# Earlier requests for raw weights, a third buffer for v pairs, and the early normalisation on GpSimd

## The chip, the core and the metric

The kernel runs on one core of a Trainium2 chip. The metric is the device time of one execution in microseconds, the median of several runs. The engines are TensorE (PE in the profile, with its weight loads as PEld), VectorE (DVE), ScalarE (ACT), GpSimd (POOL) and SyncE (SP), which here only issues DMAs. Each engine works through its own queue in order.

## What is computed

Attention with a forget bias, then two gated layers, all in fp32 accuracy (B = 4, H = 8, S = 576, D = 64; 2304 tokens of 512):

```python
scores = scale * np.matmul(q, k.transpose(0, 1, 3, 2))
cum = np.cumsum(np.maximum(s, 0.0), axis=-1)
bias = -(cum[:, :, :, None] - cum[:, :, None, :])
scores = np.where(causal, -1000000000.0, scores + np.minimum(bias, 0.0))
attn = np.exp(scores - np.max(scores, axis=-1, keepdims=True))
attn = attn / (np.sum(attn, axis=-1, keepdims=True) + 1e-09)
x = np.matmul(attn, v)                                   # then heads side by side: 2304 x 512
x = (1.0 / (1.0 + np.exp(-(x @ w_gate))) * (x @ w_val)) @ moe_w_out      # 512 -> 1536 -> 512
h = x @ w_in                                                             # 512 -> 2048
out = (h - np.tanh(h)) @ moe2_w_out                                      # -> 512
```

## The kernel before

Only the first of the kernel's stages is touched: attention together with the first gated layer, up to about 560 us of the span. The attention is cut into units, one for each batch entry, head and half G of the queries; the 32 units of G = 0 (256 queries) come first. A unit of G = 0 has two steps, t = 0 with 128 keys and t = 1 with 256, so steps 0 to 63 belong to G = 0. The first N32 = 16 units (steps 0 to 31) compute with plain fp32 operands; later units split each operand into two fp32r parts.

The order on every engine is written out by hand, in the loop over steps at line 533. Iteration i holds: on DVE eps(i-1), ttr(i) (the scores read out of PSUM with the bias and the row minimum), recip(i-1) and norm(i-1); on ACT the read-out of the transposed p of step i-2, then exp(i); on POOL mask(i+2), an affine select on the bias tile cbc; on PE qk(i+1), then the transposes tr(i-1), then pv once a unit is complete. From iteration 20 on PE also gets blocks of the first gated layer, called moe here: 12 matmuls for one 128-column weight and one group of 256 queries. Two of them go into each iteration from 20 to 28, one into those from 29 to 34. What moe writes is read out by ACT (tanh) and DVE (gt), and stored by SP in flush.

The weights come as raw 64-bit words, 24 loads of 512 KB, into tiles raw, and are turned into pairs of fp32r tiles (w00h, w00l and so on) by the class Conversion. One call of tick k does three things: for weight k-2 an ACT copy to the h part (line 109) and a POOL subtract to the l part (line 110), for weight k-1 two DVE instructions that join the words (lines 79, 80), for weight k an ACT scale that reads the raw tile (line 75). Three ticks come before the loop, then one at the end of iterations 1, 3, 5, 7, 9, 11 and 13, then one in each iteration from 15 on. Raw tiles have three buffers, and the load of weight k+1 is requested at tick k:

```python
while self.loaded < min(len(self.jobs), max(self.ticks - 1, 0) + self.nraw, most):
    self.raw[i] = self.pool.tile([128, 1024], U, tag="raw", name="raw", bufs=self.nraw)
    SP.dma_start(out=self.raw[i], in_=self.jobs[i][0])
```

SP issues in program order the q and k of a unit (kq, lines 255 and 259), the bias rows of a unit (cbc, two DMAs, line 276), the v of two heads (vpair, two DMAs, line 282), the raw weights (line 96) and the stores of gt (line 476). A load waits in SP's queue until its buffer is free, and everything behind it waits too. load_vc(u+2) asks for a vpair at the first step of an even unit u; vpair has two buffers in pool ld, so it needs pv of unit u-1 to be over:

```python
d["v"] = ld.tile([128, 2, 2, D], F, tag="v", name="vpair")
for a in range(2):
    SP.dma_start(out=d["v"][:, :, a], in_=v[b, h + a, :, 0:nj])
```

Two tiles pth and ptl in pool pt hold p for units from 16 on. POOL clears them at iterations 14 and 15; nothing else uses them before step 32. For those units split_kq makes kl, qs and split_v makes vs on POOL.

Of the kernel before, what the change touches and what calls it, by code (L numbers as in the profile page):

```python
# [8 lines left out]
F = mybir.dt.float32  # L9
R = mybir.dt.float32r  # L10
U = mybir.dt.uint32
# [3 lines left out]
B, H, S, D = 4, 8, 576, 64  # L15
# [12 lines left out]
NK = 3  # L28
# [3 lines left out]
RAW0 = 2  # L32
N32 = 16
# [14 lines left out]
def width(t):  # L48
    return Q0[t] + 128
# [6 lines left out]
def NORM(G, t):  # L56
    return "pool" if t > 2 else "dve"
# [3 lines left out]
def attention_moe_moe2(ctx: ExitStack, tc: tile.TileContext, kqT, v, s, wg, wv, wo, win, wo2, out):  # L61
    nc = tc.nc
    PE, ACT, DVE, POOL, SP = nc.tensor, nc.scalar, nc.vector, nc.gpsimd, nc.sync
# [19 lines left out]
    class Conversion:  # L83


        def __init__(self, pool, jobs, nraw, ntmp, first=99):
            self.pool, self.jobs, self.nraw, self.ntmp = pool, jobs, nraw, ntmp
            self.loaded = self.ticks = 0
            self.raw, self.tmp = {}, {}
            self.load(first)  # L90

        def load(self, most=99):
            while self.loaded < min(len(self.jobs), max(self.ticks - 1, 0) + self.nraw, most):
                i = self.loaded
                self.raw[i] = self.pool.tile([128, 1024], U, tag="raw", name="raw", bufs=self.nraw)
                SP.dma_start(out=self.raw[i], in_=self.jobs[i][0])
                self.loaded += 1

# [130 lines left out]
    pt = a_right.enter_context(tc.tile_pool(name="pt", bufs=1, side="right"))  # L229
    ld = a_right.enter_context(tc.tile_pool(name="ld", bufs=2, side="right"))  # L230
    at = a_right.enter_context(tc.tile_pool(name="at", bufs=2, side="right"))
    sm = a_right.enter_context(tc.tile_pool(name="sm", bufs=4, side="right"))
    cv = a_right.enter_context(tc.tile_pool(name="cv", bufs=2, side="right"))

    make_identity(nc, ident)
    NPT = 1
    pts = [[pt.tile([128, 5, 320], R, name=f"pt{p}{i}") for p in "hl"] for i in range(NPT)]

    units = [(b, G, h) for G in range(2) for b in range(B) for h in range(H)]
    steps = [(u, t) for u, (b, G, h) in enumerate(units) for t in GRP[G][2]]  # L240
# [2 lines left out]
    def shape(u):  # L243
        b, G, h = units[u]
        q0, qw, ts = GRP[G]
        return b, h, q0, q0 + qw, qw, 2 if G == 0 else 5
# [15 lines left out]
    def load_vc(u):  # L262
        if u >= len(units):
            return
        b, h, q0, kw, qw, nj = shape(u)
        d = U_[u]
        if u >= N32:
            d["v"] = ld.tile([128, 5, D], F, tag="v", name="vraw")[:, :nj]
        elif h % 2:
            d["v"] = U_[u - 1]["v"]  # L270
        else:
            d["v"] = ld.tile([128, 2, 2, D], F, tag="v", name="vpair")
        d["c"] = c = ld.tile([128, CW], F, tag="c", name="cbc", bufs=3)
        for t in GRP[units[u][1]][2]:
            k0 = 288 if t == 4 else 0
            SP.dma_start(out=c[:, CO[t]:CO[t] + width(t) - k0],
                         in_=cscr[b * H + h, k0:width(t)].partition_broadcast(128))
        if u >= N32:
            SP.dma_start(out=d["v"], in_=v[b, h, :, 0:nj])
        elif h % 2 == 0:  # L280
            for a in range(2):
                SP.dma_start(out=d["v"][:, :, a], in_=v[b, h + a, :, 0:nj])
# [98 lines left out]
    def norm(i):  # L381
        if 0 <= i < n:
            e = T_[i]
            u, t = steps[i]
            if NORM(units[u][1], t) == "pool":
                POOL.tensor_scalar(out=e["sp"], in0=e["sp"], scalar1=e["r"], scalar2=1.0, op0=ALU.mult, op1=ALU.mult)
            else:
                DVE.tensor_scalar(out=e["sp"], in0=e["sp"], scalar1=e["r"], scalar2=None, op0=ALU.mult)  # L388
# [121 lines left out]
    cq = [((wg, wv)[g][m].bitcast(U).rearrange("p k c -> p (k c)"), *wgv[g][m]) for m in range(M1) for g in range(2)]  # L510
# [1 line left out]
    sraw = at.tile([32, S], F, tag="sp", name="sraw", bufs=NSP)  # L512
    SP.dma_start(out=sraw, in_=s.rearrange("b h s -> (b h) s"))
    load_kq(0)
    cvt = Conversion(cv, cq, 3, 3, RAW0)
    zt = at.tile([32, S], F, tag="sp", name="zt", bufs=NSP)
    cum = at.tile([32, S], F, tag="sp", name="cumsum", bufs=NSP)
    DVE.memset(zt, 0.0)
# [1 line left out]
    DVE.tensor_tensor_scan(out=cum, data0=sraw, data1=zt, initial=0.0, op0=ALU.add, op1=ALU.add)  # L520
    SP.dma_start(out=cscr, in_=cum)
    load_vc(0)
    load_kq(1)
    load_vc(1)
    for _ in range(PRE):
        cvt.tick()
# [6 lines left out]
    for i in range(n + LN + 1):  # L533
        u, t = steps[i] if i < n else (None, None)
        b, G, h = units[u] if i < n else (None, None, None)
        first = i < n and t == GRP[G][2][0]
        if first and h == 0:
            left = (16 if G == 0 else 24) + LN + 2 + (2 if u + H == len(units) else 0)
        k = -(-len(mq) // left) if i < n else 0
# [49 lines left out]
            moe(*mq.pop(0))  # L589
        if CONV_AT(i):  # L590
            cvt.tick()
        if i in (N32 - 2, N32 - 1):
            POOL.memset(pts[0][i % 2].bitcast(F), 0.0)
    for x in xq:
        xsum(*x)
        xsplit(x[0])
# [16 lines left out]
    cvt = Conversion(cv2, [(wo[m * 128:(m + 1) * 128].bitcast(U), *won[m]) for m in range(M1)], 4, 3)  # L613
# [45 lines left out]
    jobs = [(win[m].bitcast(U).rearrange("p k c -> p (k c)"), *winn[m]) for m in range(M2)]  # L659
    cv3 = b_right.enter_context(tc.tile_pool(name="cv3", bufs=2, side="right"))  # L660
    cvt = Conversion(cv3, jobs, 2, 3)
# [114 lines left out]
    def wload(p):  # L776
# [3 lines left out]
    cvt = PairConversion(cv4, [("right", [wo2[m * 128:(m + 1) * 128].bitcast(U) for m in (p, p + MP)], p)  # L780
                               for p in range(MP)], dst, POOL)
# [60 lines left out]
    for i, (s, p) in enumerate(dsteps):  # L842
# [7 lines left out]
        for n in OORD:  # L850
            g, f = OG[n], OW[n]
# [54 lines left out]
```

## Time and profile before

| | before |
|---|---|
| median of 3 runs | 1117.04 us (1116.92 to 1117.46) |
| the profiled execution, its own time | 1119.6 us |
| its span | 1117.8 us |
| PE busy | 1061.5 us (95%) |
| DVE, ACT, POOL busy | 681.7, 546.0, 458.7 us |
| chain that ended last | PE 84%, DMA 6%, DVE 4%, ACT 2% |

The page cuts the span into 40 slices of 28 us. PE is busy in nine tenths or more of every slice from the fifth to the 39th; the first four read 3, 8, 6 and 8 tenths. What the change touches lies in these first slices.

### The profile page before, as it was taken

The numbers are of one execution on the slowest core, as the hardware profiler recorded it, in microseconds if no ns is written. First come the engines' busy times: TensorE is split into PE (matmuls) and PEld (weight loads), VectorE is DVE, ScalarE is ACT, GpSimd is POOL, SyncE is SP. The second block draws the span as 40 slices with busy tenths as digits, with TensorE's granted clock in tenths as the row PEclk, the third lists the DMA queues.
The fourth block names the chain that finished last, engine by engine and source line by source line (L and its number), as shares of the span: only waits on it lengthen the run. The fifth ranks groups of instructions, "written<-read, shape, count | busy, mean of one in ns | idle before, by whom it ended". The sixth has DMA issues, their size and how long they took to land.

```text
span 1117.8 us, 21882 instructions
## 1 busy us (share of the span) xinstructions
PE 1061.5 (95%) x7528; PEld 1023.6 (92%) x7528; DVE 681.7 (61%) x1654; ACT 546.0 (49%) x1286; POOL 458.7 (41%) x580
## 2 busy tenths in 40 slices
PE   3868999999999999999999999999999999999998
PEld 1547899989999999998999999999999999999997
DVE  4764856577867677764545654244444436778876
ACT  3543656566756566664434443344444333334333
POOL 2442645467756656662321211013333323354442
PEclk9999999999999999999999999999999999999999
DMA  5545545565756465550755563244465668644433
GB/s 186 163 139 166 153 128 146 159 186 150 178 143 173 126 185 136 157 139 24 234 177 182 168 193 111 57 143 142 135 233 197 253 230 328 236 118 140 143 89 109
DMA packets 123888, 180.38 MB, mean 161 GB/s; under 512 B 16960, under 2 KB 102464, under 8 KB 122496
## 3 DMA queue, kind: packets, MB, share of 16 engines
q1 hardware_dynamic: 123776, 178.98, 52.7%
q8 instruction: 59, 0.97, 0.4%
q14 instruction: 53, 0.43, 0.1%
HBM read 131.93 MB, written 47.00 MB: 160 GB/s over the span
## 4 chain that ended last, share of the span: by engine, by line
PE 84%; DMA 6%; DVE 4%; ACT 2%; issue 2%; SPq 1%; POOL 0%; DVEq 0%; ACTq 0%; POOLq 0%
PE bank L490 8%; PE bank L491 8%; PE bank L494 8%; PE bank L722 6%; PE bank L725 6%; PE bank L721 6%; PE bank L857 5%; PE bank L855 5%; PE bank L856 5%; PE bank L438 5%; PE bank L683 4%; PE bank L684 4%; PE bank L687 4%; PE bank L400 4%; PE bank L349 2%; DMA raw<-in_wv 2%
## 5 line engine op out<-in xcount | busy, mean ns | idle before, releaser
L857 PE MATMUL bank<-wo,sl 128*128 128x256 f32 x504 | 142.6, 283 | 0.8 <-DVE sl L770 0.8
L855 PE MATMUL bank<-wo,sh 128*128 128x256 f32 x504 | 141.9, 281 | 0.0
L856 PE MATMUL bank<-wo,sh 128*128 128x256 f32 x504 | 141.8, 281 | 0.0
L721 PE MATMUL bank<-yh,big 128*128 128x288 f32 x512 | 139.6, 294 | 0.0
L722 PE MATMUL bank<-yh,big 128*128 128x288 f32 x512 | 139.5, 295 | 0.0
L418 ACT ACTIVATE pth<-bank 128x512 fp32r<-128x512 f32 (+2 forms) x128 | 59.5, 465 | 144.0 <-PE bank L438 86.7
L728 DVE TENSOR_TENSOR th<-bank,th 128x288 f32<-128x288 f32 x128 | 57.4, 456 | 113.9 <-ACT th L727 112.3
L400 PE MATMUL bank<-ident,sp 128*128 128x128 f32 (+1 forms) x480 | 78.1, 272 | 37.0 <-DVE sp L388 15.8
L419 DVE TENSOR_TENSOR ptl<-bank,pth 128x512 fp32r<-128x512 f32 (+2 forms) x128 | 66.7, 521 | 66.5 <-PE bank L438 39.2
L400 PEld LDWEIGHTS bank<-ident,sp 128*128 128x128 f32 (+1 forms) x480 | 52.7, 143 | 55.2 <-issue 24.1
L370 ACT ACTIVATE sp<-sp,nm 128x576 f32<-128x576 f32 (+2 forms) x160 | 95.7, 598 | 13.6 <-DVE nm L363 13.6
L727 ACT ACTIVATE th<-bank 128x288 f32<-128x288 f32 x128 | 51.9, 410 | 99.8 <-PE bank L725 98.4
L857 PEld LDWEIGHTS bank<-wo,sl 128*128 128x128 f32 x504 | 95.3, 189 | 1.7 <-DVE sl L770 1.2
L722 PEld LDWEIGHTS bank<-yh,big 128*128 128x128 f32 x512 | 96.1, 188 | 0.0
L721 PEld LDWEIGHTS bank<-yh,big 128*128 128x128 f32 x512 | 96.0, 187 | 0.0
L856 PEld LDWEIGHTS bank<-wo,sh 128*128 128x128 f32 x504 | 95.3, 189 | 0.0
L855 PEld LDWEIGHTS bank<-wo,sh 128*128 128x128 f32 x504 | 95.3, 189 | 0.0
L725 PE MATMUL bank<-yl,big 128*128 128x288 f32 x512 | 88.6, 294 | 0.0
L765 POOL TENSOR_TENSOR s<-g 128x256 f32<-128x256 f32 (+1 forms) x40 | 37.1, 926 | 124.6 <-DMA g<-h 95.0
L629 DVE TENSOR_TENSOR gl<-g,gh 128x384 fp32r<-128x384 f32 x72 | 39.9, 557 | 75.9 <-PE bank L687 47.6
L388 DVE TENSOR_SCALAR sp<-sp,r 128x128 f32<-128x128 f32 (+1 forms) x96 | 81.2, 845 | 3.4
L363 DVE CUSTOM_DVE_ANT_0 sp<-bank,cbc 128x288 f32<-128x288 f32 (+2 forms) x160 | 76.1, 476 | 4.2 <-POOL cbc L327 2.6
(358 smaller groups left out, 3163.3 us busy)
## 6 DMA issues: line engine op xcount, KB each, us to landing
h<-th SPq DMA_DIRECT2D x128, 144.0 KB, 2.3
kq<-in_kq SPq DMA_DIRECT2D x32, 448.0 KB, 3.8
raw<-in_wo SPq DMA_DIRECT2D x28, 512.0 KB, 4.8
g<-g SPq DMA_DIRECT2D x72, 192.0 KB, 2.6
g<-h SPq DMA_DIRECT2D x72, 128.0 KB, 2.3
w<-wst SPq DMA_DIRECT2D x5, 1792.0 KB, 6.4
wo<-w SPq DMA_DIRECT2D x5, 1792.0 KB, 8.5
cbc<-cum SPq DMA_DIRECT2D x32, 256.0 KB, 5.5
```

The costliest lines, as they stand in the source:

```text
L370: ACT.activation(out=e["sp"], in_=e["sp"], func=AF.Exp, scale=-1.0, bias=e["m"], accum_out=e["sum"])
L388: DVE.tensor_scalar(out=e["sp"], in0=e["sp"], scalar1=e["r"], scalar2=None, op0=ALU.mult)
L400: PE.transpose(ps[:, j, :], e["sp"][p0:128, c:c + 128], ident[p0:128, p0:128])
L490: PE.matmul(ps, wh[:, c], xh[:, k], start=(k == 0), stop=False)
L491: PE.matmul(ps, wl[:, c], xh[:, k], start=False, stop=False)
L494: PE.matmul(ps, wh[:, c], xl[:, k], start=False, stop=(k == KD - 1))
L721: PE.matmul(ps, wh[:, c], Y_[blk][k][0], start=(k == 0), stop=False)
L722: PE.matmul(ps, wl[:, c], Y_[blk][k][0], start=False, stop=False)
L725: PE.matmul(ps, wh[:, c], Y_[blk][k][1], start=False, stop=(k == KD - 1))
L855: PE.matmul(o, sh[:, g, c], w[:, 0, f], start=(p == 0 and t == 0), stop=False)
L856: PE.matmul(o, sh[:, g, c], w[:, 1, f], start=False, stop=False)
L857: PE.matmul(o, sl[:, g, c], w[:, 0, f], start=False, stop=(p == MP - 1 and t == nt - 1))
```

## The change

Four edits in the first stage:

- Conversion for these weights gets two further buffers, nraw + extra = 5. The load of weight k+3 is requested at tick k. Buffers 3 and 4 of each five (rawx) lie in pool pt, in the memory of the later pth and ptl.
- pth and ptl are therefore made, and cleared on POOL, at iterations 30 and 31, after the last conversion.
- vpair moves to pool at, into the three buffers of tag kl, which units from 16 on use for kl. Tag v of pool ld is left to the v of units from 16 on.
- norm of the first 16 units (32 instructions) is issued on POOL, in front of mask(i+2), in the form that later steps with t > 2 already use there.

```diff
-        def __init__(self, pool, jobs, nraw, ntmp, first=99):
-            self.pool, self.jobs, self.nraw, self.ntmp = pool, jobs, nraw, ntmp
+        def __init__(self, pool, jobs, nraw, ntmp, first=99, more=None, extra=0):
+            self.pool, self.jobs, self.nraw, self.ntmp = pool, jobs, nraw + extra, ntmp
+            self.more, self.own = more, nraw
...
-                self.raw[i] = self.pool.tile([128, 1024], U, tag="raw", name="raw", bufs=self.nraw)
+                k = i % self.nraw - self.own
+                if k < 0:
+                    self.raw[i] = self.pool.tile([128, 1024], U, tag="raw", name="raw", bufs=self.own)
+                else:
+                    self.raw[i] = self.more.tile([128, 1024], U, tag=f"pt{'hl'[k]}", name="rawx")
...
-            d["v"] = ld.tile([128, 2, 2, D], F, tag="v", name="vpair")
+            d["v"] = at.tile([128, 2, 2, D], F, tag="kl", name="vpair", bufs=NK)
...
-            if NORM(units[u][1], t) == "pool":
+            if u < N32 or NORM(units[u][1], t) == "pool":
...
-    cvt = Conversion(cv, cq, 3, 3, RAW0)
+    cvt = Conversion(cv, cq, 3, 3, RAW0, pt, 2)
...
-        if i in (N32 - 2, N32 - 1):
-            POOL.memset(pts[0][i % 2].bitcast(F), 0.0)
+        if i in (2 * N32 - 2, 2 * N32 - 1):
+            assert cvt.done(len(cq) - 1)
+            p = "hl"[i % 2]
+            pts[0].append(pt.tile([128, 5, 320], R, tag=f"pt{p}", name=f"pt{p}0"))
+            POOL.memset(pts[0][-1].bitcast(F), 0.0)
```

The order of instructions on PE is the same in both kernels, and so is that on ACT apart from the names of two buffers. On DVE 32 norms go. SP and POOL are shown at three places; in the changed file the line numbers are five higher, and eight from the loop's end on.

On SP, at the start of the program: the q and k of units 1 to 3 (kq), bias rows (cbc), v pairs and raw weights. Before:

```order
L255 DMA kq_201<-in_kq 64x512
L276 DMA cbc<-cum 128x128
L276 DMA cbc<-cum 128x256
L96 DMA raw<-in_wg 128x1024
L96 DMA raw<-in_wv 128x1024
L255 DMA kq_238<-in_kq 64x512
L276 DMA cbc<-cum 128x128
L276 DMA cbc<-cum 128x256
L282 DMA vpair<-in_v 128x2x64 x2
L96 DMA raw<-in_wg 128x1024
L255 DMA kq_286<-in_kq 64x512
```

And of the change:

```order
L260 DMA kq_199<-in_kq 64x512
L281 DMA cbc<-cum 128x128
L281 DMA cbc<-cum 128x256
L101 DMA raw<-in_wg 128x1024
L101 DMA rawx<-in_wv 128x1024
L101 DMA rawx<-in_wg 128x1024
L101 DMA raw<-in_wv 128x1024
L260 DMA kq_240<-in_kq 64x512
L281 DMA cbc<-cum 128x128
L281 DMA cbc<-cum 128x256
L287 DMA vpair<-in_v 128x2x64 x2
L101 DMA raw<-in_wg 128x1024
```

Four raw loads now stand ahead of what unit 2 needs (kq_238, now kq_240, and its cbc), where two stood.

On POOL, in iterations 2 to 5, masks (cbc), weight subtracts (w01l, w11l) and, in the change, the norms (sp). Before:

```order
L327 AFFINE_SELECT cbc<-cbc 128x128 x2
L110 TENSOR_TENSOR w01l<-tmp,w01h 128x512
L327 AFFINE_SELECT cbc<-cbc 128x128 x2
L110 TENSOR_TENSOR w11l<-tmp,w11h 128x512
L327 AFFINE_SELECT cbc<-cbc 128x128 x2
```

And of the change:

```order
L391 TENSOR_SCALAR sp<-sp,r 128x128
L332 AFFINE_SELECT cbc<-cbc 128x128
L115 TENSOR_TENSOR w01l<-tmp,w01h 128x512
L391 TENSOR_SCALAR sp<-sp,r 128x256
L332 AFFINE_SELECT cbc<-cbc 128x128
L391 TENSOR_SCALAR sp<-sp,r 128x128
L332 AFFINE_SELECT cbc<-cbc 128x128
L115 TENSOR_TENSOR w11l<-tmp,w11h 128x512
L391 TENSOR_SCALAR sp<-sp,r 128x256
```

A norm now stands behind the mask of the iteration before it, and behind the weight subtract when that iteration has a tick.

On POOL, in iterations 30 to 32, with kl and qs of unit 17 and 18, the last weight subtract w111l and the clearing of pth and ptl. Before:

```order
L297 TENSOR_TENSOR kl<-kq,kh 128x256
L301 TENSOR_TENSOR qs<-kq,qs 64x256
L110 TENSOR_TENSOR w111l<-tmp,w111h 128x512
L327 AFFINE_SELECT cbc<-cbc 128x128 x2
L315 TENSOR_TENSOR vs<-vraw,vs 128x2x64
L297 TENSOR_TENSOR kl<-kq,kh 128x256
```

And of the change:

```order
L391 TENSOR_SCALAR sp<-sp,r 128x256
L332 AFFINE_SELECT cbc<-cbc 128x128
L302 TENSOR_TENSOR kl<-kq,kh 128x256
L306 TENSOR_TENSOR qs<-kq,qs 64x256
L115 TENSOR_TENSOR w111l<-tmp,w111h 128x512
L601 MEMSET pth_1452 128x1600
L391 TENSOR_SCALAR sp<-sp,r 128x128
L332 AFFINE_SELECT cbc<-cbc 128x128
L601 MEMSET ptl_1490 128x1600
L391 TENSOR_SCALAR sp<-sp,r 128x256
```

The clearing has moved from between masks of iterations 14 and 15 to a place where the norms of steps 30 and 31 stand right behind it.

## Rows read from the trace of the kernel before

**Rows 1.** SP's waits, 0 to 135 us: total us, times, longest us.
```profile
SPq L282 <- PE bank L430: 35.1, 6, 10.1
```

**Rows 2.** Timeline around 65 us: start, us, instruction, count, [idle before <-releaser].
```profile
63.01 0.90 SPq L282 DMA_DIRECT2D vpair<-in_v  x2
64.01 0.40 SPq L96 DMA_DIRECT2D raw<-in_wg  x1
...
68.01 0.66 ACT L75 ACTIVATE tmp<-raw 128x512 f32<-128x512 f32 x1 [5.73 <-DMA raw<-in_wg]
...
68.89 0.69 PE L400 MATMUL bank<-ident,sp 128*128 128x128 f32 x2 [4.77 <-ACT p L413]
```

**Rows 3.** ACT's waits, 10 to 135 us: total us, times, longest us.
```profile
ACT tmp L75 <- DMA raw<-in_wg: 34.5, 7, 9.8
```

**Rows 4.** Timeline of PE, 20 to 76 us: pv of units 0, 1 and 8, first moe.
```profile
24.17 1.49 PE L430 MATMUL bank<-p,vpair 128*128 128x256 f32 x4
...
28.35 1.49 PE L430 MATMUL bank<-p,vpair 128*128 128x256 f32 x4
...
73.52 1.51 PE L430 MATMUL bank<-p,vpair 128*128 128x256 f32 x4
...
76.11 0.58 PE L490 MATMUL bank<-xh,w00h 128*128 128x256 f32 x1
```

**Rows 5.** PE by shape, 10 to 76 us: busy us, mean ns | idle before.
```profile
L341 PE MATMUL bank<-kq 64*128 64x256 f32 x20 | 12.2, 712 | 0.0
```

**Rows 6.** PE by shape, 76 to 133 us.
```profile
L341 PE MATMUL bank<-kq 64*128 64x256 f32 x11 | 4.1, 446 | 0.0
```

**Rows 7.** Timeline of PE, 85 to 140 us: rows after idle, and two transposes.
```profile
90.67 0.44 PE L400 MATMUL bank<-ident,sp 128*128 128x128 f32 x2 [2.59 <-ACT p L413]
...
111.45 0.53 PE L400 MATMUL bank<-ident,sp 128*128 128x128 f32 x2 [2.38 <-ACT p L413]
...
130.00 0.27 PE L400 MATMUL bank<-ident,sp 128*128 128x128 f32 x1
...
134.33 0.27 PE L400 MATMUL bank<-ident,sp 128*128 128x128 f32 x1
...
138.92 0.33 PE L400 MATMUL bank<-ident,sp 128*128 128x128 f32 x1 [1.55 <-DVE ptl L419]
```

**Rows 8.** Stretches: length, busy of PE, PEld, DVE, ACT, POOL, PEclk, DMA share, GB/s.
```profile
92.00:96.00 4.00, 4.00 (x23) 3.65 (x23) 3.33 (x9) 2.40 (x7) 2.07 (x2) 0.68 0.68 206
...
112.00:116.00 4.00, 3.90 (x19) 3.56 (x20) 3.75 (x9) 2.46 (x6) 2.07 (x2) 0.62 0.80 249
```

**Rows 9.** DVE by shape, 10 to 76 us: busy us, mean ns | idle before.
```profile
L388 DVE TENSOR_SCALAR sp<-sp,r 128x256 f32<-128x256 f32 x10 | 11.2, 1116 | 0.4
L80 DVE SCALAR_TENSOR_TENSOR tmp<-raw,tmp 128x512 uint32<-128x512 uint32 x12 | 9.2, 770 | 0.4
L79 DVE TENSOR_SCALAR tmp<-tmp 128x512 uint32<-128x512 uint32 x13 | 5.5, 420 | 1.1 <-ACT tmp L75 1.1
```

**Rows 10.** POOL by shape, 10 to 76 us.
```profile
L327 POOL TENSOR_SCALAR_AFFINE_SELECT cbc<-cbc 128x128 f32<-128x128 f32 x23 | 7.7, 344 | 15.1 <-DMA cbc<-cum 15.1
...
L593 POOL MEMSET pth<- 128x1600 f32 x1 | 1.4, 1432 | 0.1
...
L110 POOL TENSOR_TENSOR w02l<-tmp,w02h 128x512 fp32r<-128x512 f32 x1 | 1.3, 1347 | 2.5 <-ACT w02h L109 2.5
```

**Rows 11.** DVE by shape, 76 to 133 us.
```profile
L388 DVE TENSOR_SCALAR sp<-sp,r 128x256 f32<-128x256 f32 x6 | 2.6, 441 | 0.2
```

**Rows 12.** POOL by shape, 76 to 133 us.
```profile
L297 POOL TENSOR_TENSOR kl<-kq,kh 128x256 fp32r<-128x256 f32 x3 | 2.2, 739 | 3.4 <-ACT kh L296 3.4
```

**Rows 13.** POOL by shape, 300 to 500 us.
```profile
L386 POOL TENSOR_SCALAR sp<-sp,r 128x576 f32<-128x576 f32 x21 | 15.8, 751 | 1.4 <-DVE r L379 1.2
L386 POOL TENSOR_SCALAR sp<-sp,r 128x512 f32<-128x512 f32 x22 | 15.3, 697 | 13.5 <-DVE r L379 11.0 <-PE bank L438 2.3
```

**Rows 14.** POOL's waits, 10 to 135 us: total us, times, longest us.
```profile
POOL cbc L327 <- DMA cbc<-cum: 15.1, 10, 3.4
```

More of the change, by code (lines that the diff above doesn't have):

```diff
@@ L236, in attention_moe_moe2 @@
     NPT = 1
-    pts = [[pt.tile([128, 5, 320], R, name=f"pt{p}{i}") for p in "hl"] for i in range(NPT)]
+    pts = [[]]
     units = [(b, G, h) for G in range(2) for b in range(B) for h in range(H)]
```

## Prediction

> **What bounds the kernel now.** I read the page's slices first: PE is full from about 112 us to the end, and its instructions stand in the same order in both kernels. So the time changes by what PE loses before about 140 us: idle time, and time at the lower clock. Next come SP's waits, since SP issues every load in order. Its two vpair loads waited 35.1 us in six places for pv on PE [rows 1]: with two buffers a pair asked for at unit u needs pv of unit u-1. The timeline shows what hangs on that [rows 2]. The vpair goes out at 63.01, the raw weight behind it only at 64.01; ACT, in order, has by then sat 5.73 us when its scale starts at 68.01, behind it stands the read-out of p, and PE has been idle 4.77 us at 68.89. ACT lost 34.5 us in seven such waits [rows 3], the longest, 9.8 us, being the start of the kernel, which stays.
>
> Two stretches differ. **Up to the first moe (76.11 us)** PE has attention alone. Without a stall a unit takes it 28.35 - 24.17 = 4.18 us, pv to pv [rows 4]; 2.09 us a step. PE shows no idle time between these two rows, so there PE itself is the limit, at its slow clock: the same 64x256 matmul takes 712 ns there and 446 ns later [rows 5, 6]. The page prints the full granted clock for these early slices, and the durations contradict it. **From 76 us** PE has moe besides and is full but for two raw stalls, 2.59 and 2.38 us, and one of 1.55 us [rows 7]. After each of the first two the granted clock falls from 2.4 to 1.2 GHz for a while: 0.68 in 92 to 96 us, 0.62 in 112 to 116 [rows 8].
>
> **The change, part by part.**
>
> *The stalls that go, early.* With three buffers a vpair needs pv of unit u-3, over some three steps before the request. Raws are asked for two ticks earlier, four steps where ticks come every other step. So I let all raw stalls after the start go. From pv of unit 0 to pv of unit 8 are 8 x 4.18 = 33.4 us, and from there to the first moe 76.11 - 73.52 = 2.6 [rows 4]: the first moe could start at 24.17 + 33.4 + 2.6 = 60.2 instead of 76.11, **15.9 us** earlier. Next late is PE itself.
>
> *What takes some of that back.* (a) At the start four raws stand ahead of unit 2's q, k and bias where two stood. Two raws are 1.05 MB; DMA moved 249 GB/s when 80% busy [rows 8], 311 at full, so that is 3.4 us. The floor is 0, if the transfers hide behind the 9.8 us that ACT waits anyway. Mask(4) then waits on POOL, and norm(2) behind it. I take **2**.
>
> (b) The norm on POOL. Its shapes of 512 and 576 columns take 697 and 751 ns [rows 13], 0.84 ns a column, so 128 and 256 columns come to 0.37 and 0.48 us by extension. On DVE the 256-column norm took 1116 ns in this stretch, where it meets POOL's subtract, and 441 later [rows 9, 11]: I read this as VectorE and GpSimd holding each other up. I therefore add what shares that path. For two steps with one tick: norms 0.37 + 0.48, masks 2 x 0.34, one subtract 1.35, L79 0.42, L80 0.77 [rows 9, 10]: 4.07 us against PE's 4.18. Hidden, barely; a norm queued behind a subtract comes as late as DVE's norm did when the subtract held it up. The bounds are 0 and some 0.3 us for each of seven units, 2; I take **1**. What DVE saves by losing the norm is worth nothing there, since PE is the limit.
>
> (c) From iteration 15 every step has a tick: 0.43 + 0.34 + 1.35 + 0.42 + 0.77 = 3.3 us a step against 2.09. Four such iterations precede the first moe: at most 4 x 1.2 = 4.8, at least 0, if the lag stays in queues. I take **3**, near the top, because the norm stands behind the subtract in one queue.
>
> The first stretch gives 15.9 - 2 - 1 - 3 = **9.9 us**.
>
> *The stalls that go, from 76 us.* 2.59 + 2.38 = 5.0 us idle. At the lower clock PE lost (1 - 0.68) x 4.00 + (1 - 0.62) x 3.90 = 2.8 us [rows 8]. Together **7.8 us**. At worst one of the two stays, and 3.9 are left. The slow first moes stay, since PE comes to them from the same slow stretch. With two moes a step PE is full, 4.00 of 4.00 us, beside DVE at 3.33 and POOL at 2.07 [rows 8]; moving 0.4 us a step from one to the other keeps both below PE.
>
> *Iterations 30 to 32.* The 1.55 us idle [rows 7] comes from a late kq, queued on SP behind the v of later units, which shared buffers with vpair. It should go. In its place POOL has in iteration 30: norm 0.48, mask 0.34, kl 0.74, qs about as much, subtract 1.35, memset 1.43 [rows 10, 12, 13]: 5.1 us, while a step with one moe takes PE (134.33 - 130.00)/2 = 2.2 [rows 7]. The norm of step 30 stands behind the memset. With some 1.5 us of slack between a norm and its transposes, a guess, I charge 5.1 - 2.2 - 1.5 = 1.4, and 0.3 for the rest: **1.7**, between 0 and 3.5. kl of unit 18 also waits on POOL for pv of unit 15, whose buffer it takes; one mask is queued behind it, needed two steps later, so that costs nothing. Net: 1.55 - 1.7 = -0.15.
>
> Dropping the clearing at iterations 14 and 15 gives nothing by itself, as PE is the limit there without stalls.
>
> *Sum:* 9.9 + 7.8 - 0.15 = 17.5 us. The profiled execution took 1119.6 us, 1.8 outside its span of 1117.8, and 2.6 above the median. I subtract from the median: 1117.04 - 17.5 = **1099.5**; a profiled span would be near 1100.3. With every charge at its floor, below which none has a reason to go, the gain is 15.9 + 7.8 + 1.55 = 25.2 (1091.8); with all at their tops, and one middle stall left, it is 15.9 - 3.4 - 2 - 4.8 + 3.9 + 1.55 - 3.5 = 7.7 (1109.4).
>
> **Rivals.**
>
> *A. POOL's queue becomes the pace.* Norm, mask and subtract stand in one queue, and DVE's norm at 1116 ns shows what a meeting of the two costs [rows 9]. With moe a norm has the same 1.5 us of slack; if waits of both engines use that up, each of the 14 steps from 20 to 33 loses say 0.5 us: 7 us, giving **1106.5**. For it: DVE is busy 3.33 of 4.00 us already [rows 8]. Against it: POOL is busy only 2.07. Chance 0.15.
> The Trainium skill, "GPSIMD Engine Reference", section 4.1 (Engine selection), sends elementwise work on a tile to VectorE and calls GpSimd about twice as slow for two inputs, near line rate for one. My rows put the norm between the two, 0.48 against 0.44 us. At twice DVE's time the two norms of a unit would cost about 0.8 us more than mine, an estimate; over seven early units that is 5.6 us, and the sum would be 1105.
>
> *B. The clock rises early.* With PE never stalled the attention stretch could reach 2.4 GHz. The limit is then the 4.07 us of (b) for a unit, less what hides; six units save up to 0.4 us each, and the first two moes, slow now, about 1 us each: 4.5 us, **1095**. Against it: PE had no idle time between 24.17 and 28.35 and stayed slow. Chance 0.08.
> The Trainium skill, "TensorE: Matmul & The Clock Gate", Part 1, says that sustained activity releases the throttle; this trace's attention stretch does not bear that out.
>
> *C. Slower: masks hold the norms.* Mask(i+2) waits for a cbc load, and now a norm stands behind it. POOL waited for cbc 15.1 us in ten places [rows 14], 1.5 us each, so far for free. More raws ahead of cbc lengthen that. If each of 14 units pays 1.5 us of it on the path, 21 us: 1117.04 - 17.5 + 21 = **1120.5**. It decides from 17.5/14 = 1.25 us a unit. Against it: the waits come from SP's vpair stalls, which go, and cbc is then asked for about three steps ahead. Chance 0.06.
>
> *D. Raws stay late.* SP still waits for the join of weight k-2 before it requests weight k+3, into the same buffer. If it sets the requests, nothing moves: **1117**. Against it: the request then serves a tick three later, not the next. Chance 0.05.
>
> **How the numbers follow.** Forecast 0.64 (1092 to 1108), A 0.15, B 0.08, C 0.06, D 0.05, better than all floors 0.02. The range 1092 to 1110 takes in the forecast, B and most of A, about 8.5 in 10. A measurement here tells about 0.2% (2.2 us) from no change. Faster: 0.64 + 0.15 + 0.08 + 0.02 = 0.89; within 0.2%: D, 0.05; slower: C, 0.06.
>
> **What would show it.** Right: no wait of SP's vpair for pv, no wait of ACT for raws after the start, first moe near 66 us, no PE idle between it and iteration 30, no granted clock under 1 around 90 and 112 us. A start later than 70 us with POOL releasing PE's transposes speaks for (b), (c) or A; POOL waits on cbc followed by PE idle for C. The prediction is wrong if the first moe does not come earlier, or if PE, freed of raws, idles behind norms with moe running.

## The result, and the profile after

Measured beside each other, the kernel before took 1117.25 us (four runs, 1116.92 to 1117.64) and the changed one 1100.34 us (1099.35 to 1100.66): a ratio of 0.9847, 95% interval 0.983 to 0.9864, 16.9 us less. The prediction was 1099.5 us, between 1092 and 1110. The profiled execution of the changed kernel took 1100.66 us, 1098.9 of it span. L405 is now the line of the transposes that was L400. One execution in the experiments, the first of e1, took 2599.5 us, nearly all of it busy PE, and is left out.

The page of the changed kernel, its row of PE in 40 slices:

```profile
PE   3999999999999999998999999999999999999998
```

PE is full, or nearly, from the second slice (27 us) on. The waits of SP from 0 to 135 us, changed kernel (total us, times, longest us), its four largest:

```profile
SPq L101 <- DVE tmp L80: 12.5, 5, 3.9
SPq L481 <- DVE tmp L79: 12.0, 4, 4.5
SPq L481 <- DVE gt L511: 9.9, 5, 2.7
SPq L284 <- POOL vs L320: 7.6, 4, 4.5
```

The wait of vpair for pv on PE, 35.1 us before [rows 1], is gone. So is every wait of ACT for a raw weight after 24 us; that was 32.6 us in eleven places before, 24.7 of them among those of [rows 3] and 7.9 for the loads from in_wv, which [rows 3] leaves out. What SP waits for now are raw buffers (L101), with weights asked for so early that nobody waits for them, and results that it is to store (L481).

PE's timeline in the changed kernel (start, length, instruction, count, [idle before <- releaser]): pv of units 0, 1 and 8, the transposes after idle time, the first row of the first two moes, and the transposes of steps 29 to 34:

```profile
24.45 1.49 PE L435 MATMUL bank<-p,vpair 128*128 128x256 f32 x4
28.64 1.49 PE L435 MATMUL bank<-p,vpair 128*128 128x256 f32 x4
...
54.84 0.48 PE L405 MATMUL bank<-ident,sp 128*128 128x128 f32 x1 [1.13 <-POOL sp L391]
...
60.84 0.47 PE L405 MATMUL bank<-ident,sp 128*128 128x128 f32 x1 [1.75 <-POOL sp L391]
61.10 1.49 PE L435 MATMUL bank<-p,vpair 128*128 128x256 f32 x4
...
63.67 0.58 PE L495 MATMUL bank<-xh,w00h 128*128 128x256 f32 x1
...
66.49 0.36 PE L495 MATMUL bank<-xh,w10h 128*128 128x256 f32 x1
...
105.58 0.38 PE L405 MATMUL bank<-ident,sp 128*128 128x128 f32 x2
...
110.17 0.33 PE L405 MATMUL bank<-ident,sp 128*128 128x128 f32 x1 [2.53 <-POOL sp L391]
...
114.20 0.38 PE L405 MATMUL bank<-ident,sp 128*128 128x128 f32 x2
...
116.09 0.27 PE L405 MATMUL bank<-ident,sp 128*128 128x128 f32 x1
...
118.52 0.38 PE L405 MATMUL bank<-ident,sp 128*128 128x128 f32 x2
...
119.83 0.33 PE L405 MATMUL bank<-ident,sp 128*128 128x128 f32 x1 [0.69 <-DVE ptl L424]
```

A unit takes 28.64 - 24.45 = 4.19 us, as before [rows 4]. The first moe starts at 63.67 instead of 76.11. From there PE has no idle time until 107.6 us. Then comes a stall that was not there before: 2.53 us in front of the transposes of step 30. Its other side is POOL's timeline, changed kernel, 104 to 110 us:

```profile
104.00 0.48 POOL L391 TENSOR_SCALAR sp<-sp,r 128x256 f32<-128x256 f32 x1 [1.07 <-DVE r L384]
104.43 0.29 POOL L332 TENSOR_SCALAR_AFFINE_SELECT cbc<-cbc 128x128 f32<-128x128 f32 x1
105.48 0.75 POOL L302 TENSOR_TENSOR kl<-kq,kh 128x256 fp32r<-128x256 f32 x1 [0.75 <-ACT kh L301]
106.30 0.74 POOL L306 TENSOR_TENSOR qs<-kq,qs 64x256 fp32r<-64x256 f32 x1
107.12 1.27 POOL L115 TENSOR_TENSOR w111l<-tmp,w111h 128x512 fp32r<-128x512 f32 x1
108.33 1.43 POOL L601 MEMSET pth<- 128x1600 f32 x1
109.73 0.38 POOL L391 TENSOR_SCALAR sp<-sp,r 128x128 f32<-128x128 f32 x1
```

The reciprocal for step 30 was ready on DVE at 106.14 us. The norm waited 3.6 us more, behind two splits, the last weight subtract and the first clearing. The stretches around it, changed kernel (length, busy of PE, PEld, DVE, ACT, POOL, PEclk, DMA share, GB/s):

```profile
108.00:112.00 4.00, 1.83 (x9) 1.73 (x10) 0.04 (x1) 1.38 (x6) 4.00 (x6) 0.83 0.36 108
112.00:116.00 4.00, 4.00 (x28) 4.00 (x28) 2.50 (x11) 1.62 (x6) 2.83 (x7) 0.74 0.17 53
```

From 108 to 112 us POOL is busy all the time, DVE for 0.04 us, and the granted clock falls to 0.83 and 0.74. This is the pattern of the two raw stalls before [rows 8], with another cause.

### The profile page after: what moved, and what is told of

It reads as the page before. It is cut to its first block, busy times and chain, and to the rows that moved or that the text cites. A ratio compares the mean times of both kernels' runs of the same rounds, so it can differ in the third digit from the quotient of the medians.

```text
span 1098.9 us, 21882 instructions
## 1 busy us (share of the span) xinstructions
PE 1058.2 (96%) x7528; PEld 1021.5 (93%) x7528; DVE 667.6 (61%) x1622; ACT 546.0 (50%) x1286; POOL 469.7 (43%) x612
## 4 chain that ended last, share of the span: by engine, by line
PE 81%; DVE 4%; DMA 2%; issue 1%; ACT 1%; SPq 0%; POOL 0%; DVEq 0%; ACTq 0%; POOLq 0%
PE bank L495 8%; PE bank L499 8%; PE bank L496 8%; PE bank L730 6%; PE bank L733 6%; PE bank L729 6%; PE bank L865 5%; PE bank L443 5%; PE bank L691 5%; PE bank L692 5%; PE bank L695 5%; PE bank L863 4%; PE bank L864 4%; PE bank L405 4%; PE bank L354 2%; PE bank L355 2%
## 5 line engine op out<-in xcount | busy, mean ns | idle before, releaser
L405 PE MATMUL bank<-ident,sp 128*128 128x128 f32 (+1 forms) x480 | 78.1, 272 | 22.4 <-POOL sp L391 13.5
L405 PEld LDWEIGHTS bank<-ident,sp 128*128 128x128 f32 (+1 forms) x480 | 52.7, 143 | 40.2 <-POOL sp L391 22.5
L391 POOL TENSOR_SCALAR sp<-sp,r 128x512 f32<-128x512 f32 (+1 forms) x96 | 60.2, 627 | 57.8 <-DVE r L384 48.4
```

The lines of the kernel that those rows point to most:

```text
L405: PE.transpose(ps[:, j, :], e["sp"][p0:128, c:c + 128], ident[p0:128, p0:128])
```

## The parts of the change, each alone and in pairs

The change has three parts that can be taken apart: v pairs in three buffers (V), raws three ahead in five buffers (R), norms on GpSimd (N). The clearing at iterations 30 and 31 belongs to R, since the raws use that memory. All eight combinations were timed. One mark on PE serves to compare them: its first row that waits for ptl, at 138.92 us before [rows 7] and at 119.83 after. "To mark" is from the first moe to it, "rest" from it to the end of the span; all times in us. In the four series of experiments the kernel before had medians from 1117.66 to 1119.87 us, so ratios compare better than medians.

| parts | run | ratio to before, 95% | first moe | to mark | rest |
|---|---|---|---|---|---|
| none | before | 1 | 76.11 | 62.81 | 978.9 |
| V | e5 | 0.9799 (0.9782 to 0.9816) | 64.90 | 52.80 | 976.7 |
| R | e2 | 0.9853 (0.9819 to 0.9886) | 63.34 | 58.28 | 977.7 |
| N | e3 | 1.0042 (1.0027 to 1.0056) | 76.32 | 65.30 | 978.8 |
| V, R | e4 | 0.9784 (0.9756 to 0.9812) | 63.20 | 52.87 | 978.1 |
| R, N | e6 | 0.9936 (0.9914 to 0.9958) | 69.08 | 60.79 | 978.6 |
| V, N | e7 | 0.9841 (0.9826 to 0.9855) | 65.45 | 53.60 | 979.7 |
| V, R, N | after | 0.9847 (0.983 to 0.9864) | 63.67 | 56.16 | 979.1 |

**V alone.** The edit, against the kernel before:

```diff
-            d["v"] = ld.tile([128, 2, 2, D], F, tag="v", name="vpair")
+            d["v"] = at.tile([128, 2, 2, D], F, tag="kl", name="vpair", bufs=NK)
```

> The kernel before, with one line changed: the v pairs rotate through the three buffers of tag kl. Theory Queue (SP standing at the vpair loads is the whole cause of the late raw weights): SP no longer waits for pv on PE, ACT's raw waits after the start go, and most of the 17 us is here already, about 1103 us. Theory Depth (a raw weight asked for one tick ahead is too late whatever stands in front of it): SP's waits go, but ACT's raw waits shrink only in part, first moe between 68 and 74 us, 1107 to 1114 us. Theory Both-needed: under 2 us from this part alone, 1115 to 1117.

Its ratio was 0.9784 (0.9751 to 0.9817), a median of 1095.2 us.

> The same kernel as in e1_vpair_only (the one changed line of the v pairs), run again for a trace at the usual pace, since the one of e1 lasted 2598 us. Theory Queue: 1094 to 1097 us; SP has no wait for pv; ACT waits for no raw weight after the start; the first moe starts at 63 to 64 us, and from there to the transposes of step 29 PE loses nothing. Theory Depth would want raw waits of 1 us or more left on ACT in the stretch with a tick in every step, and 2 us or more between this and the kernel after without its norms (1094.8).

1095.58 us. Theory Queue holds in the total and in SP's waits, whose largest in this kernel are now, from 0 to 135 us:

```profile
SPq L96 <- DVE tmp L80: 19.4, 10, 4.4
SPq L476 <- DVE tmp L79: 10.9, 5, 4.1
SPq L255 <- PE bank L341: 7.8, 7, 1.7
```

It missed its numbers, first: e1 was to come to 1103 and came 8 us lower. And it missed in one place, where theory Depth was right: ACT still waits 3.2 us for raws after 24 us, in two places (2.45 and 0.72 us). Neither is followed by idle time of PE. The first moe starts at 64.90, not before 64. **One changed line gives the whole gain, and some 5 us more than all of the change.**

**R alone.** The edit, in the kernel after:

```diff
-            d["v"] = at.tile([128, 2, 2, D], F, tag="kl", name="vpair", bufs=NK)
+            d["v"] = ld.tile([128, 2, 2, D], F, tag="v", name="vpair")
...
-            if u < N32 or NORM(units[u][1], t) == "pool":
+            if NORM(units[u][1], t) == "pool":
```

> The kernel after, with the v pairs back in their two buffers and all early norms back on DVE: only the raw weights three ticks ahead in five buffers are left of the change, and with it the clearing at iterations 30 and 31. Theory Queue: SP still waits some 35 us for pv, the raws are still late, 1112 to 1117 us. Theory Depth: SP waits as long as before, but the request now serves a tick two later, so ACT's raw waits go; first moe near 64 us; about 1097 to 1103 us. With no norm behind the clearing on POOL, the stall near 110 us should be missing too.

1102.19 us: theory Depth, to its upper end. SP still waits for pv, and hardly anybody waits for a raw. SP's longest wait in this kernel, from 0 to 135 us:

```profile
SPq L287 <- PE bank L435: 24.3, 6, 5.9
```

And ACT's waits for raws, from 24 to 135 us:

```profile
ACT tmp L75 <- DMA rawx<-in_wg: 1.2, 1, 1.2
ACT tmp L75 <- DMA raw<-in_wg: 1.1, 1, 1.1
```

So V and R cure the same stall, one at the request, one by asking earlier, and in the total the second adds nothing that can be told from noise: V with R is 0.9784, V alone 0.9784 and 0.9799. The traces do show a gain up to the first moe, 63.20 against 64.90 us. Half of it is the clearing, which R moves away from iterations 14 and 15. DVE's, POOL's and PE's rows there in V alone (e5):

```profile
50.56 2.39 DVE L388 TENSOR_SCALAR sp<-sp,r 128x256 f32<-128x256 f32 x1
...
51.37 1.43 POOL L593 MEMSET ptl<- 128x1600 f32 x1
...
53.09 0.66 PE L400 MATMUL bank<-ident,sp 128*128 128x128 f32 x2 [0.87 <-DVE sp L388]
```

The norm lasts until the clearing is over, and PE idles 0.87 us; e4 has no idle time there.

What R alone lacks against V with R is 5.4 us between the first moe and the mark. PE there has five idle rows, the longest 2.92 us for ptl. SP asks for a kq only at 116.65 us, behind a v load (L284) that waits 7.1 us for its buffer, and ACT, in order, waits 1.18 us for this v and 1.14 for the kq in front of pth. The v pairs share these buffers again, as they did where PE idled 1.55 us before [rows 7].

**N alone.** The edit, against the kernel before:

```diff
-            if NORM(units[u][1], t) == "pool":
+            if u < N32 or NORM(units[u][1], t) == "pool":
```

> The kernel before, with one line changed: the norms of the first 32 steps run on GpSimd. Theory PE-bound (DVE's time is worth nothing where PE or the raws set the pace): 1117 us, plus or minus 1.5. Theory Relief (DVE's norm at 1.1 us beside GpSimd was on the path): 1112 to 1115 us. Theory Masks (a norm stands behind a mask that waits for its late cbc, which it does while SP still stands at vpair): 1119 to 1122 us, with PE idle behind GpSimd's sp.

1122.87 against 1118.42 us in the same series: just past the upper end of theory Masks, but its mechanism is the smaller part. It is there once: a mask waits 3.20 us for its bias rows, the norm stands behind it (38.29), and PE idles 2.43 us at 38.71. Yet the first moe comes only 0.2 us later than before. The mark comes 2.5 us later than that, and the largest new idle row is that of step 30:

```profile
132.63 0.33 PE L400 MATMUL bank<-ident,sp 128*128 128x128 f32 x1 [1.75 <-POOL sp L386]
```

Its norm stands behind two splits and a subtract on POOL (129.31 to 132.22 us), with no clearing near. The norm on GpSimd never pays. It costs 0.0042 alone and with V, 0.0063 with V and R, 0.0083 with R.

**V and R, without N.** The edit: the second half of the diff of e2, in the kernel after.

> The kernel after, with the early norms back on DVE. Theory Clearing (the 19.1 us shift would be 22.5 but for the norms of steps 30 and 31 standing behind the two memsets on GpSimd): PE's idle 2.5 us at 110 us and the lower clock behind it go, and the time falls by 3 to 4 us against the kernel after, to about 1096.5 to 1097.5 us. Theory Relief (GpSimd's norm shortens the early steps): the first moe comes later than 63.7 us, by 1 to 3 us, and the total stays at 1099 to 1102 us. Theory Neither: 1100.3 us within 1.

1094.84 us: under the changed kernel by 0.0063 of the kernel before (some 7 us), and by 4.7 us in the spans of the two traces, more than theory Clearing said. The stall at 110 us is gone, as that theory has it: from the transposes of step 29 (106.08 us here) to the mark are 9.99 us, in the changed kernel 119.83 - 105.58 = 14.25. Theory Relief is out: the first moe came earlier here, not later.

**R and N, without V.** The edit: the first half of that diff, in the kernel after.

> The kernel after, with the v pairs back in their two buffers: raws three ahead and norms on GpSimd are left. Theory Clearing (the norm costs only where it stands behind the two memsets): raws alone gave 1102.2, plus 3 to 4 us for the stall near 110 us, 1105 to 1106.5 us. Theory Norm (each meeting of norm and subtract on GpSimd costs, clearing or not): 1107 to 1110 us, with PE idle behind GpSimd's sp in other places too. Theory Hidden (SP's vpair waits and the norm's stall overlap): 1101 to 1103 us.

1110.86 us: just past theory Norm, and by the mechanism that the prediction called C. The timeline of this kernel, three of POOL's rows and the PE row that they release:

```profile
58.32 0.29 POOL L332 TENSOR_SCALAR_AFFINE_SELECT cbc<-cbc 128x128 f32<-128x128 f32 x1 [3.16 <-DMA cbc<-cum]
58.58 1.26 POOL L115 TENSOR_TENSOR w14l<-tmp,w14h 128x512 fp32r<-128x512 f32 x1
...
59.82 0.37 POOL L391 TENSOR_SCALAR sp<-sp,r 128x128 f32<-128x128 f32 x1
...
60.25 0.48 PE L405 MATMUL bank<-ident,sp 128*128 128x128 f32 x1 [3.36 <-POOL sp L391]
```

The mask waits 3.16 us for its bias rows, which stand on SP behind a vpair that waits for pv. The subtract and the norm stand behind the mask, and PE idles 3.36 us. The norm turned a wait that was free [rows 14] into a stall; in the changed kernel, with V, POOL waits only 4.1 us in all for these rows, in five places. The first moe comes 5.7 us later than in R alone. From there to the mark another 2.5 us are lost, with 3.50 us of idle time in front of step 30 (119.33).

**V and N, without R.** The edit: both diffs, of V and of N, in the kernel before; the clearing stays at iterations 14 and 15.

> The kernel before, with the v pairs in three buffers and the early norms on GpSimd, but with three raw buffers and the clearing at iterations 14 and 15 as before. Theory Clearing: no memset stands ahead of the norms of steps 30 and 31, so the stall near 110 us goes; the time is that of the v pairs alone plus some 0.5 us, 1095 to 1096.5 us; the memsets at 14 and 15 meet early norms and may cost up to 2 us there. Theory Norm: it keeps what the kernel after loses, 1099 to 1101 us.

1099.97 us: theory Norm by the total, though not for its reason. The norm of step 30 still comes late, now without a clearing in front of it. POOL's and PE's rows in this kernel:

```profile
107.59 0.74 POOL L297 TENSOR_TENSOR kl<-kq,kh 128x256 fp32r<-128x256 f32 x1 [0.75 <-ACT kh L296]
108.42 0.74 POOL L301 TENSOR_TENSOR qs<-kq,qs 64x256 fp32r<-64x256 f32 x1
109.23 1.27 POOL L110 TENSOR_TENSOR w111l<-tmp,w111h 128x512 fp32r<-128x512 f32 x1
110.48 0.37 POOL L386 TENSOR_SCALAR sp<-sp,r 128x128 f32<-128x128 f32 x1
...
110.91 0.33 PE L400 MATMUL bank<-ident,sp 128*128 128x128 f32 x1 [1.16 <-POOL sp L386]
```

Two splits and a subtract are enough for 1.16 us of idle time. No lower clock follows it: 1.00 from 108 to 124 us. Against V alone the spans differ by 4.3 us: 0.55 at the first moe, 0.80 up to the mark, 2.95 behind it, where both have the same instructions in the same order (see the last section).

## Where the norm costs, and where it doesn't

**The clearing moved behind the norms.** The edit, in the kernel after:

```diff
-        if i in (2 * N32 - 2, 2 * N32 - 1):
+        if i == 2 * N32:
...
-            p = "hl"[i % 2]
+            for p in "hl":
```

> The kernel after, with both memsets issued at the end of iteration 32, behind the norms of steps 30 and 31 (first use of the cleared tiles: read-out of step 32 in iteration 34). Theory Clearing: PE's idle 2.5 us at 110 us goes, the later marks come 3 to 4 us earlier, 1096 to 1097.5 us. Theory Norm: the gain is under 1 us, 1099.5 us or more. A new wait could come: the read-out of step 32 behind 2.9 us of memsets, PE idle behind ptl or pth near 120 us, up to 2 us.

1098.22 us, ratio 0.9825 (0.9811 to 0.984): between the two theories. PE's idle time before step 30 falls from 2.53 to the same 1.16 us as in e7, and the late read-out that was named as a risk costs 1.14 instead of 0.69 us. From the first moe to the mark are 54.19 us, between the changed kernel's 56.16 and e4's 52.87. The parts show between the transposes of step 29 and the mark: 9.99 us in e4, 11.35 in e7 with no clearing there, 12.11 here, 14.25 in the changed kernel. So the splits and the subtract cost 1.4 us, the clearing in front of the norm 2.9 more, and behind it still 0.8.

**The norms of steps 30 and 31 back on DVE, the other 30 left on GpSimd.** The edit, in the kernel after:

```diff
-            if u < N32 or NORM(units[u][1], t) == "pool":
+            if (u < N32 and i < 2 * N32 - 2) or NORM(units[u][1], t) == "pool":
```

> The kernel after, with the norms of steps 30 and 31 alone back on DVE; the 30 before them stay on GpSimd and the memsets stay where they are. Theory Place (the early norms cost nothing while PE is the limit; the whole price is paid at step 30, where the norm stands behind two splits, a subtract and a memset): 1094.5 to 1097 us, no PE idle behind sp after 66 us, first moe still at 63.5 to 64 us. Theory Norm (each norm on GpSimd costs a little): at most half of the 5.5 us comes back, 1097.5 us or more.

1096.41 us, ratio 0.9793 (0.9774 to 0.9812), inside the interval of e4: theory Place. On DVE the norm of step 30 starts at 106.74 us and takes 0.29; in the changed kernel it starts at 109.73. From the first moe to the mark are 52.61 us, against 52.87 with all norms on DVE and 56.16 in the changed kernel. Thirty norms on GpSimd cost nothing, two cost the 3.5 us up to the mark.

**Fewer ticks before the first moe.** In V alone, R and V with R the early idle time of PE is there too, with norms on DVE: 1.33 and 1.65 us in e4 where the changed kernel has 1.13 and 1.75. PE's rows in e4:

```profile
54.51 0.45 PE L405 MATMUL bank<-ident,sp 128*128 128x128 f32 x1 [1.33 <-DVE sp L393]
...
60.38 0.45 PE L405 MATMUL bank<-ident,sp 128*128 128x128 f32 x1 [1.65 <-DVE sp L393]
```

So the norm's engine does not make it; the tick in every step may. The edit, against V alone:

```diff
-    return i in CS or i > 14
+    return i in CS or i in (15, 17) or i > 18
```

> The kernel of e1 and e5 (v pairs alone), with the conversion ticks of iterations 16 and 18 left out, so that ticks come every other step until iteration 19 and the last two weights are ready two iterations later. Theory Ticks (the 4 us that PE idles between 53 and 62 us come from a tick in every step, which keeps DVE busy 18.3 of 19 us there): PE's idle in that stretch falls below 1 us, the first moe comes 2 to 4 us earlier, near 61.5 us, and the total is 1092 to 1094 us. Theory Given back: the last subtracts then meet the splits of the first units with p tiles, near iteration 32, and PE idles there: 1095 to 1097 us.

1097.53 us, ratio 0.9799 (0.9781 to 0.9817): no gain over V alone, in the way that theory Given back describes, a little past its range. The first moe came 3.8 us earlier, at 61.13. From there to the mark it took 57.02 us instead of 52.80, since the last ticks now meet the splits. DVE's and POOL's rows of this kernel, and the PE row behind them:

```profile
106.63 1.38 DVE L388 TENSOR_SCALAR sp<-sp,r 128x128 f32<-128x128 f32 x1
106.67 1.27 POOL L110 TENSOR_TENSOR w110l<-tmp,w110h 128x512 fp32r<-128x512 f32 x1
...
108.16 0.30 PE L400 MATMUL bank<-ident,sp 128*128 128x128 f32 x1 [1.73 <-DVE sp L388]
```

A norm that takes DVE 0.29 us when GpSimd is free takes 1.38 beside the subtract.

**The same with two ticks in iterations 20 and 21,** where two moes fill PE, so that the last weight is ready as early as in the changed kernel. The edit beside that of e10, made in the kernel of e4, and for e12 in that of e9:

```diff
-        if CONV_AT(i):
-            cvt.tick()
+        for _ in range(2 if i in (20, 21) else CONV_AT(i)):
+            cvt.tick()
```

> The kernel of e4 (v pairs and raws, norms on DVE) with the ticks of iterations 16 and 18 moved to iterations 20 and 21, which then make two each; the last weight is ready at iteration 30, as in the kernel after. Theory Ticks: as in e10 PE's idle before the first moe falls below 1 us and the first moe starts near 60.5 to 61.5 us; with the last subtracts out of the way of iteration 32 nothing is given back: 0.976 of the kernel before, 2 to 3 us under e4's ratio of 0.9784. Theory Given back: DVE and GpSimd cannot take two ticks in a step beside two moes, PE idles behind sp or p near iterations 20 to 22: no gain over e4.

> The kernel of e9 (norms on GpSimd but for steps 30 and 31) with the same two ticks moved to iterations 20 and 21. Theory Relief: here DVE has room (12.9 of 19 us busy before the first moe in e9, 18.3 with its norms in e5), so the two ticks per step fit and the early idle goes, first moe near 61.5 us: 0.976 of the kernel before, at or below e11. Theory Norm: GpSimd, with 15.9 of 19 us busy there, is the one that has no room, PE idles behind its sp near iterations 20 to 22, and the time is e9's ratio of 0.979 or more.

1093.73 us with norms on DVE (ratio 0.9777, 0.9761 to 0.9794) and 1093.86 with the first 30 on GpSimd (0.9783, 0.9763 to 0.9803). In the traces theory Ticks holds in both: from 32.2 us to the mark PE has no idle row in either, so in e12 theory Norm is out, and Relief is not needed, since e11 does as well without it. In e11 the first moe starts at 60.03, the mark comes at 113.43 us, 2.6 before e4's 116.07. The 2 to 3 us under e4's ratio that theory Ticks forecast do not show in the total. Both beat the kernel before by 2.2%. By their intervals they can't be told from e4, e5 or e9, but they stand 0.6 to 0.7% under the changed kernel.

## The prediction, step by step

The total was right: 1099.5 forecast, 1100.34 measured. Its terms were less so: two gains were put 2.5 and 2.3 us too low and one cost 3.6 us too low. That the total came within a microsecond is in part luck.

| term | forecast, us | measured, us |
|---|---|---|
| (a) more raws at the start | +2 (0 to 3.4) | +0.28 (pv of unit 0 at 24.45, was 24.17) |
| (b) norm sharing POOL, early | +1 (0 to 2) | 0 |
| (c) a tick in every step | +3 (0 to 4.8) | +2.9 (1.13 and 1.75 idle) |
| up to the first moe | -9.9 | -12.4 |
| raw stalls from 76 us | -7.8 | -10.1 |
| iterations 30 to 32 | -0.15 | +3.4 |
| sum | -17.5 | -19.1 at the mark, -18.9 in the span |

**What went, and why: right.** Most signs that were named are there: no wait of vpair for pv, no late raw, the first moe near 66 (63.67), no idle time from there to iteration 30, no low clock at 90 us. Two went the other way. The granted clock around 112 us is under 1 (0.83 and 0.74), and PE, freed of raws, idles 2.53 us behind a norm with moe running, which the prediction had named as a sign of being wrong. Both belong to the term of iterations 30 to 32. The step that 15.9 us can be had before the first moe holds too: 15.9 less 0.28 and 2.9 is 12.7, and 12.44 came. What the prediction did not ask is whether one part alone would have done it.

**(a) and (b) were charged for nothing.** pv of unit 0 lies at 23.88 us in e4 and 24.62 in e9, which ask for the same raws, so (a) is not larger than this scatter. From there to the first moe are 39.22 us in the changed kernel and 39.32 in e4, with norms on DVE: (b) is 0, its floor. The 4.07 us against PE's 4.18 were enough. A term that the prediction put at nothing, the dropped clearing at iterations 14 and 15, does count where the norm is on DVE: 0.87 us of idle time in e5.

**(c) was sized right with a wrong reason.** It was put near the top "because the norm stands behind the subtract in one queue". With the norm on DVE the same 3 us are lost (e4), and with the ticks spread none, on either engine (e11, e12). The tick is the cause; where the norm stands is not.

**The stalls from 76 us gave 2.3 us more than charged.** The transposes of step 29 came at 105.58, before at this place:

```profile
128.10 0.38 PE L400 MATMUL bank<-ident,sp 128*128 128x128 f32 x2
```

That is 22.5 us earlier, 10.1 of it after the first moe. One microsecond comes from the first two moes, which were said to stay slow: only the first did, 4.84 us for the two instead of 5.83. (In e4 both were slow, so this is not the change's own.) The lower clock before was also undercounted: beside the stretches of [rows 8], the granted clock was 0.90 in 88 to 92 us and 0.96 in 108 to 112, 0.6 us more. With 0.22 us of idle time at 91.33, some 0.5 us stay untraced.

**Iterations 30 to 32 is the term that was wrong.** The sum put 5.1 us of POOL work against 2.2 us of a step and "some 1.5 us of slack between a norm and its transposes, a guess". The work was there as listed, 4.6 us from the start of kl to the end of the norm. The step that failed is taking off a whole step of 2.2 us: when the reciprocal was ready, at 106.14, only 0.66 us of this work was over. The guess itself was good, since PE ran out of work 1.5 us later, at 107.64. So 2.53 us of idle time came, not 1.7. Behind it the step from 110.17 to 114.20 took 4.03 us, the same sequence one unit later 2.43 (116.09 to 118.52): 1.6 us at the lower clock, which the working had charged for the raw stalls and forgot here. Against this stand 0.86 us less before the mark (0.69 idle where there were 1.55). The bound of 3.5 was passed by some 0.7. That splits and subtract do 1.2 us of the idle time with no clearing in front of the norm, e7 and e8 show.

**The gap between profile and median.** The difference of the profiled executions is 18.9 us, that of the medians 16.9. The profiled execution before, 1119.6 us, lay 2.4 above the median measured beside the change, the one after 0.3 above its own. Subtracting the sum from the median hid this: 17.5 from a median of 1117 looks exact, but the same sum was 1.6 us short of what the traces show.

**The rivals.** *A*, POOL as the pace, did not come as priced: PE lost nothing in the steps up to 29, and then 2.53 us in one, where four long instructions stand in a row. Nor did the estimate of 1105 at twice DVE's time: GpSimd's norms took 0.38 and 0.48 us, against 0.29 and 0.35 on an undisturbed DVE, and cost nothing before the first moe. *B*, the clock rising early, did not come: in e11 PE has no idle time from 32.16 to 60.03 us, and the pair of 64x256 matmuls at 58.88 still takes 1.22 us, 0.70 once moe has run for a while (e5, 105.58), much the gap between [rows 5] and [rows 6]. The Trainium skill, "TensorE: Matmul & The Clock Gate", Part 1, says that sustained activity releases the throttle; none of these traces shows it in this stretch. *C*, norms held behind masks, is what e6 does, and e3 in one place; the argument put against it, that vpair's stalls go, is what kept the changed kernel from it. *D* is out: no raw is late.

## What to carry over

When two edits attack the same wait, price each as if the other were made: here the second was worth 1.7 us up to the first moe and nothing that the total shows, and its clearing was paid in full. Before moving a small instruction on the path to another engine, look for the place where that engine's longest instructions stand in a row, since here the one worst place set the price, not the mean load. A stall of a full PE can be charged twice, as idle time and as the lower clock behind it. With moe running, the stalls of 2.38 to 3.50 us up to 145 us were all followed by a granted clock under 1; the shorter ones, 1.75 us at most (e3 at 132.63, e10 at 108.16, e7 and e8 in front of step 30), were not.

## What the runs showed of the hardware

**A DVE norm beside GpSimd.** The norm of step 31 in e4, on DVE, and then two of GpSimd's rows at that time:

```profile
107.94 2.24 DVE L393 TENSOR_SCALAR sp<-sp,r 128x256 f32<-128x256 f32 x1
```

```profile
107.38 1.28 POOL L115 TENSOR_TENSOR w111l<-tmp,w111h 128x512 fp32r<-128x512 f32 x1
108.60 1.44 POOL L601 MEMSET pth<- 128x1600 f32 x1
```

The norm of 256 columns, 0.35 us where GpSimd is idle (e5, at 106.03), began inside the subtract and ended 0.14 us after the clearing: held for two instructions. The Trainium skill, "SBUF — State Buffer", section "Who interferes with whom", says that VectorE in its two-port modes, which a tensor_scalar can enter, contends with GpSimd for a shared pair of ports: whoever issues first has it for the whole instruction, and the other blocks. This trace agrees, as far as being held goes: 2.24 us instead of 0.35. PE lost nothing by it, as the norm ended just in time for the transposes at 110.40.

**The same stall, with and without a lower clock.** Where the units of the other half of the queries begin, between 200 and 240 us, every kernel has short stalls of PE; for one row they are 1.56 us in e11 (208.23) and 1.57 in e12 (208.72). The stretch behind it, e11 and then e12 (columns as above):

```profile
208.00:212.00 4.00, 3.77 (x20) 3.71 (x21) 3.72 (x11) 2.29 (x6) 3.73 (x6) 0.60 0.79 178
```

```profile
208.00:212.00 4.00, 2.99 (x25) 2.72 (x25) 3.96 (x11) 2.78 (x8) 3.92 (x6) 1.00 0.75 221
```

One falls to 1.2 GHz for part of it, the other stays at 2.4. Before, after, e7, e8 and e11 fall there; e2, e3, e4, e5, e6, e9, e10 and e12 do not. It costs about 1.6 us, (1 - 0.60) x 4, and is part of why the "rest" of the table goes from 976.7 to 979.7. It isn't the norm's engine: with all early norms on DVE the clock falls in before and e11 but not in e2, e4, e5 and e10, with all on GpSimd in after, e7 and e8 but not in e3 and e6. Each kernel has one trace, and the mean granted clock of e7's four executions already runs from 0.996 to 0.998, so whether the kernel or the execution decides stays open. So does what else differs in "rest", since kernels that do not fall range from 976.7 to 978.8, and with both the 3 us between e5 and e7.
